# Full-array first-layer products for the first two blocks of a convolution and maxout kernel

## The chip, the cores and the metric

The kernel runs on one core of a Trainium2 chip. The core has four engines that compute: TensorE (PE in the profile; PEld is its loading of weights), VectorE (DVE), ScalarE (ACT) and GpSimd (POOL). SyncE (SP) issues most of the DMAs. SBUF is the core's memory of 128 partitions, PSUM the memory into which TensorE accumulates. The metric is the time of one execution on the device in microseconds (us), as the median of several runs; lower is better.

## The reference

The input x has 8 sequences of 4160 tokens with 192 channels. A causal convolution of width 7 is applied per channel, with weights that a softmax gives for each of 8 heads of 24 channels. A feed-forward layer follows: three matrices of 192 x 768, the largest of the three products for each element, and a matrix of 768 x 192.

```python
# cut to what is computed
w = softmax(weight, axis=-1)                       # 8 heads x 7 taps
x_pad = concatenate([zeros((B, 6, D)), x], axis=1) # causal
out[b, s, h*24 + g] = sum_k w[h, k] * x_pad[b, s + k, h*24 + g]
h = maximum(maximum(out @ w1, out @ w2), out @ w3) # 33280 x 768
return h @ w_out                                   # 33280 x 192
```

## The kernel before

The 33,280 tokens are cut into 65 blocks of 512. With y the convolved block, the kernel uses max(a, b, c) = c + max(a - c, b - c, 0): it computes only the two products y(w1 - w3) and y(w2 - w3), takes relu of the first, then the larger of that and the second, and adds y(w3 w_out) at the end by a merged matrix m16 = w3 w_out.

The 192 channels are three chunks of 64. A product with 64 rows fills half of the 128-row array, so two run beside each other, one in each half: half 0 does w1 - w3, half 1 does w2 - w3. For that, each half of the partitions needs all three chunks of y. The convolution gives each chunk in one half, and the other half is a copy.

The first four blocks are "dense": their convolution (`conv_dense`) leaves channels on partitions at once. The copies into the other half are `cross` (VectorE) and, for block 3, `cross_dma`.

```python
    def conv_dense(t, copies):
        yd = dense[t] = ydp.tile([P, NC, NBLK], FP16, tag="yd", name=f"yd_{t}")   # NC = 3
        for n, slots_ in enumerate((range(4), range(4, 6))):
            ps = psw.tile([P, NBLK], FP32, tag="w", name=f"D{n}_{t}")
            for (q, b, row_lo, rlen, lo, hi, cc) in chunks_of[t]:                 # 5 of up to 103 tokens
                for v in range(2):
                    for g, s in enumerate(slots_):
                        h = (32 * s + 31 * v) // GRP
                        nc.tensor.matmul(ps[32 * g:32 * g + 32, lo:hi], ...)      # L347
            if n == 0:
                copies[0](out=yd[0:HALF, 0, :], in_=ps[0:HALF, :])                # L353
                copies[1](out=yd[HALF:P, 1, :], in_=ps[HALF:P, :])                # L354
            else:
                copies[2](out=yd[0:HALF, 2, :], in_=ps[0:HALF, :])                # L356

    def cross(t, cs=range(NC)):
        for c in cs:
            a, b = (slice(HALF, P), slice(0, HALF))[::-1 if c == 1 else 1]
            nc.vector.tensor_copy(out=yd[a, c, :], in_=yd[b, c, :])               # L363
```

From block 4 on, the convolution (`conv`, L328) leaves tokens on partitions. Its result is written to SBUF as ys (`evac`, L376) and turned by DMA transposes (`turn`, L390). Then the halves are exchanged by `double` (L400): by DMA for blocks 4 and 5, and by GpSimd after that. Blocks 5 and 6 share one turn and one doubling, so do 7 and 8, and so on up to 16; block 4 has its own. Loads of x (`load_x`, L153) and casts (`cast_x`, L183) run some blocks ahead.

```python
    def double(t, by_dma=False):
        yp = dense[t]
        copy = nc.sync.dma_start if by_dma else nc.gpsimd.tensor_copy
        for i in range(2):
            copy(out=yp[HALF * i:HALF * (i + 1), 1, ...], in_=yp[HALF * (1 - i):HALF * (2 - i), 0, ...])
```

The first layer `l1(t, j)` makes 128 of the 768 columns of one block: three 512-column products in each half. ScalarE's relu and VectorE's maximum follow (L482, L483). The second layer `st2` (L532) does 60 products of 192 columns a block; ScalarE and VectorE add its halves (L540, L541).

```python
        for c in range(NC):
            for i in range(2):
                nc.tensor.matmul(ps[i][:], lhsT=wd[HALF * i:HALF * (i + 1), c, P * j:P * (j + 1)],
                                 rhs=y_all(t, i, c), start=(c == 0), stop=(c == NC - 1))   # L475
        # then: r = relu(ps[0]) on ScalarE, h = max(r, ps[1]) on VectorE
```

In the start of the kernel, x of blocks 0 and 1 and the weights are loaded in three parts of 256 columns, the weight differences wd are made, and the layers of blocks 0 and 1 are interleaved. `keep_warm` are matmuls on zeros.

```python
    def load_w(part):
        for st, lo, wsrc in ((w3s, 0, moe_w3), (ws, 0, moe_w1), (ws, HALF, moe_w2)):
            nc.sync.dma_start(out=st[lo:lo + HALF, :, f], in_=...)                # 64 x 3 x 256, L213
    # order on SyncE: load_x(0), load_w(0), load_x(1), load_w(1), load_w(2), wos (L224), load_x(2..5)
    ...
    copy_w3(nc.vector.tensor_copy, 0);  make_wd(0, 1)                             # L284, L280
    conv_dense(0, (ACT, ACT, ACT));     keep_warm(2)
    cross(0, (0,));  make_wd(1, 2, nc.gpsimd);  cross(0, (1, 2))
    cast_dense(1, ...);  copy_w3(nc.vector.tensor_copy, 1);  l1(0, 0)
    conv_dense(1, (ACT, ACT, ACT));  cross(1);  make_wd(2, 4)
    ...                                        # l1 of blocks 0 and 1, casts and transposes of w3
    nc.gpsimd.tensor_copy(out=wo[:], in_=wos[:])                                  # L619
    load_x(6), load_x(7);  l1(0, 5);  make_m(0);  make_m(1)
    cast_dense(2);  l1(1, 4);  st2(0, (5, 5))
    conv_dense(2, ...);  cast_dense(3);  cast_x(4);  cross(2);  l1(1, 5)
    for u in range(1, 6): st2(0, (5 * u + 5, 5 * u + 5))
    ...
    # block 2: after l1(2, 0): conv_dense(3), cross_dma(3), load_x(8), conv(4), evac, turn(4), load_x(9), casts 5, 6
    # block 3: double(4, by DMA), load_x(10), casts 7, 8; after l1(3, 1): conv(5) for blocks 5 and 6, turn(5)
    # block 4: double(5, by DMA), load_x(11), ...
```

Of the kernel before, what the change touches and what calls it, by code (L numbers as in the profile page):

```python
# [28 lines left out]
def kernel(  # L29
# [177 lines left out]
    w3s = const.tile([P, NC, DFF], FP32)  # L207
    PW = 2 * P

    def load_w(part):  # L210
        f = slice(PW * part, PW * (part + 1))
        for st, lo, wsrc in ((w3s, 0, moe_w3), (ws, 0, moe_w1), (ws, HALF, moe_w2)):
            nc.sync.dma_start(out=st[lo:lo + HALF, :, f],  # L213
                              in_=wsrc.rearrange("(c r) f -> r c f", r=HALF)[:, :, f])
# [5 lines left out]
    load_w(0)  # L220
    load_x(1)
    load_w(1)
    load_w(2)
# [5 lines left out]
    for t in range(2, 6):  # L229
        load_x(t)  # L230
# [24 lines left out]
    nc.scalar.activation(out=line[:, 31:31 + KW], in_=wexp[:], func=AF.Relu, scale=wrec[:])  # L255
# [3 lines left out]
    CUT = 25  # L259
    for lo, hi, copy in ((0, CUT, nc.scalar.copy), (CUT, WIN, nc.vector.tensor_copy)):  # L260
        bps = psq.tile([32, hi - lo, NHEAD], FP32, tag="q", name=f"band_{lo}")
        for c in range(lo, hi):
            nc.tensor.matmul(bps[:, c - lo, :], lhsT=line[:, WIN - 1 - c:WIN + 31 - c],
                             rhs=ident16[0:NHEAD, 0:NHEAD], start=True, stop=True)
        for a in range(4):
            copy(out=band[32 * a:32 * a + 32, :, 32 * a + lo:32 * a + hi],
                 in_=bps[:].rearrange("p c h -> p h c"))
    keep_warm(3, psp, "p")
# [3 lines left out]
    w3h = const.tile([HALF, NC, DFF], FP16)  # L272
    wd = const.tile([P, NC, DFF], FP16)
# [4 lines left out]
    def make_wd(j0, j1, eng=nc.vector):  # L278
        f = slice(P * j0, P * j1)
        eng.tensor_sub(out=wd[:, :, f], in0=ws[:, :, f], in1=w3s[:, :, f])  # L280

    def copy_w3(copy, part):
        f = slice(PW * part, PW * (part + 1))
        copy(out=w3s[HALF:P, :, f], in_=w3s[0:HALF, :, f])  # L284

    def cast_w3(part):
        f = slice(PW * part, PW * (part + 1))
        nc.gpsimd.tensor_copy(out=w3h[:, :, f], in_=w3s[0:HALF, :, f])

    def transpose_w3(g):  # L290
        ps = psw.tile([P, 2, D], FP32, tag="w", name=f"pt{g}")
        for k in range(2):
            js = slice(P * (2 * g + k), P * (2 * g + k + 1))
            for c in range(NC):
                nc.tensor.matmul(ps[:, k, HALF * c:HALF * (c + 1)], lhsT=w3h[:, c, js],
                                 rhs=ident16[0:HALF, 0:HALF], start=True, stop=True)
        nc.scalar.copy(out=w3t[:, 2 * g:2 * g + 2, :], in_=ps[:])
# [39 lines left out]
    def conv_dense(t, copies):  # L337


        yd = dense[t] = ydp.tile([P, NC, NBLK], FP16, tag="yd", name=f"yd_{t}")  # L340
        for n, slots_ in enumerate((range(4), range(4, 6))):
            ps = psw.tile([P, NBLK], FP32, tag="w", name=f"D{n}_{t}")
            for (q, b, row_lo, rlen, lo, hi, cc) in chunks_of[t]:
                for v in range(2):
                    for g, s in enumerate(slots_):
                        h = (32 * s + 31 * v) // GRP
                        nc.tensor.matmul(  # L347
                            ps[32 * g:32 * g + 32, lo:hi],
                            lhsT=xz[t][v][0:rlen, q, 32 * s:32 * s + 32],
                            rhs=band[0:rlen, h, cc:cc + hi - lo],  # L350
                            start=(v == 0), stop=(v == 1), tile_position=(0, 32 * g))
            if n == 0:
                copies[0](out=yd[0:HALF, 0, :], in_=ps[0:HALF, :])  # L353
                copies[1](out=yd[HALF:P, 1, :], in_=ps[HALF:P, :])  # L354
            else:
                copies[2](out=yd[0:HALF, 2, :], in_=ps[0:HALF, :])  # L356

    def cross(t, cs=range(NC)):

        yd = dense[t]  # L360
        for c in cs:
            a, b = (slice(HALF, P), slice(0, HALF))[::-1 if c == 1 else 1]
            nc.vector.tensor_copy(out=yd[a, c, :], in_=yd[b, c, :])  # L363

    def cross_dma(t):
        yd = dense[t]
        nc.sync.dma_start(out=yd[HALF:P, 0:NC:2, :], in_=yd[0:HALF, 0:NC:2, :])
        nc.sync.dma_start(out=yd[0:HALF, 1, :], in_=yd[HALF:P, 1, :])
# [24 lines left out]
    def double(t, by_dma=False):  # L393

        if not NDENSE <= t < NB:
            return
        yp = dense[t]
        copy = nc.sync.dma_start if by_dma else nc.gpsimd.tensor_copy
        for i in range(2):
            copy(out=yp[HALF * i:HALF * (i + 1), 1, :, :, :, :].rearrange("p i u k n -> p (i u k n)"),  # L400
                 in_=yp[HALF * (1 - i):HALF * (2 - i), 0, :, :, :, :].rearrange("p i u k n -> p (i u k n)"))
# [11 lines left out]
    def y_all(t, i, c):  # L413
        if t < NDENSE:
            return dense[t][HALF * i:HALF * (i + 1), c, :]
        a = y_row(t, i)
        s0, s1, s2, s3 = (spot(t, i, c, r) for r in range(4))
        assert s3 - s2 == s1 - s0
        return bass.AP(tensor=a.tensor, offset=a.offset + P * s0,
                       ap=[list(a.ap[0]), [P * (s2 - s0), 2], [P * (s1 - s0), 2], [1, P]])  # L420

    def y_tok(t, i, c, s):
        if t < NDENSE:
            return dense[t][HALF * i:HALF * (i + 1), c, P * s:P * (s + 1)]
        a = y_row(t, i)
        return bass.AP(tensor=a.tensor, offset=a.offset + P * spot(t, i, c, s), ap=[list(a.ap[0]), [1, P]])
# [38 lines left out]

    def l1(t, j, pools=((psp, "p"), (psq, "q"))):
# [4 lines left out]
        def product(i, c):  # L471
            if c == 0:
                pool, tag = pools[i]
                ps[i] = pool.tile([P, NBLK], FP32, tag=tag, name=f"l{tag}{i}_{t}_{j}")
            nc.tensor.matmul(ps[i][:], lhsT=wd[HALF * i:HALF * (i + 1), c, P * j:P * (j + 1)],  # L475
                             rhs=y_all(t, i, c), start=(c == 0), stop=(c == NC - 1))

        def top():
            if t not in hs:
                hs[t] = hp.tile([P, NJ, NBLK], FP16, tag="h", name=f"h_{t}")  # L480
            r = rp.tile([P, NBLK], FP16, tag="r", name=f"r_{t}_{j}")
            nc.scalar.activation(out=r[:], in_=ps[0][:], func=AF.Relu)  # L482
            nc.vector.tensor_max(out=hs[t][:, j, :], in0=r[:], in1=ps[1][:])  # L483
            done[t] = j + 1
# [4 lines left out]
        op(top)  # L489
        emit()  # L490

# [88 lines left out]
    copy_w3(nc.vector.tensor_copy, 0)  # L580
    make_wd(0, 1)
    conv_dense(0, (nc.scalar.copy, nc.scalar.copy, nc.scalar.copy))
    keep_warm(2)
    cross(0, (0,))
    make_wd(1, 2, nc.gpsimd)
    cross(0, (1, 2))
    cast_dense(1, (nc.gpsimd.tensor_copy, nc.scalar.copy))
    copy_w3(nc.vector.tensor_copy, 1)
    l1(0, 0)
    meet()  # L590
    cast_w3(0)
    conv_dense(1, (nc.scalar.copy, nc.scalar.copy, nc.scalar.copy))
    cross(1)
    make_wd(2, 4)
    l1(0, 1)
    meet()
    keep_warm(2)
    l1(1, 0)
    meet()
    cast_w3(1)  # L600
    l1(1, 1, WW)
    meet()
    transpose_w3(0)
    copy_w3(nc.gpsimd.tensor_copy, 2)
    l1(0, 2)
    meet()
    cast_w3(2)
    transpose_w3(1)
    make_wd(4, 6, nc.gpsimd)
    l1(0, 3, WW)  # L610
    meet()
    transpose_w3(2)
    l1(1, 2)
    meet()
    l1(1, 3, WW)
    meet()
    l1(0, 4)
    meet()
    nc.gpsimd.tensor_copy(out=wo[:], in_=wos[:])  # L619
    for t in (6, 7):  # L620
        load_x(t)
    l1(0, 5, WW)
    meet()
    make_m(0)
    make_m(1)
    cast_dense(2, (nc.gpsimd.tensor_copy, nc.gpsimd.tensor_copy))
    l1(1, 4)
    meet()
    st2(0, (5, 5))
    meet()  # L630
    conv_dense(2, (nc.scalar.copy, nc.vector.tensor_copy, nc.scalar.copy))
    cast_dense(3, (nc.gpsimd.tensor_copy, nc.gpsimd.tensor_copy))
    cast_x(4)
    cross(2)
    l1(1, 5)
    meet()
    for u in range(1, NJ):
        st2(0, (5 * u + 5, 5 * u + 5))
        meet()
# [7 lines left out]
    for t in range(5, NB):  # L647
        casts[t] = min(NB - 1, casts[t - 1] + (2 if t in (6, 9, 12) else 1))
    loads = {t: min(NB - 1, casts.get(t + 1, 0) + 1) for t in range(4, NB)}
    loads.update({2: 9, 3: 10, 4: 12})  # L650
# [9 lines left out]
    for t in range(2, NB):  # L660
        u = convs_at.get(t, NB)
        late = t > 2 and u < NB
        if t in (3, 4):
            double(t + 1, True)
        if t in (3, 4):
            load_x(t + 7)
# [4 lines left out]
        if t == 2:  # L671
            meet()
            conv_dense(3, (nc.scalar.copy, nc.vector.tensor_copy, nc.scalar.copy))
            cross_dma(3)
            load_x(8)
# [4 lines left out]
            load_x(9)  # L680
# [8 lines left out]
        else:  # L689
            op(lambda t=t: store(t - 2, 0, 4, (nc.sync,)))  # L690
# [54 lines left out]
```

## Time and profile before

| | |
|---|---|
| median of 3 runs | 459.82 us (458.68 to 460.01) |
| span of the profiled run | 458.7 us |
| TensorE busy | 449.6 us, 98% |
| VectorE, ScalarE, GpSimd busy | 359.8, 318.9, 203.4 us |
| granted TensorE clock | 1.00 over the whole span |
| TensorE busy in 25-30, 40-45, 50-55 us | 4.21, 4.11, 3.98 us of 5 |
| the same in 80-85 and 85-90 us | 5.00 and 5.00 of 5 |

A line of the timeline gives start and length in us, the engine (SPq is SyncE's queue of DMA issues), the line of the source, the operation, and the tiles it writes and reads, with the number of instructions merged. A bracket at its end is the idle time of the engine just before it and who ended it. In the chain of waits a piece is start, length and what the end of the program was waiting for at that time. A busy TensorE isn't a TensorE at its peak, since matmuls overlap: the time between the starts of two is what counts.

### The profile page before, as it was taken

To read this page: it belongs to the slowest core of one execution; us is meant where nothing else is said; L and a number is where in the kernel's file an instruction comes from. 1 tells how busy PE (TensorE), PEld (TensorE's weight loads), DVE (VectorE), ACT (ScalarE), POOL (GpSimd) and SP (SyncE) were. 2 spreads that over 40 slices of the span, in tenths; PEclk is the share of its full clock that TensorE was granted. 3 is DMA by queue.
4 is the path that set the end of the run, shared out by engine and by line. 5 is a ranking of instruction groups with operands and counts; after the bars stand their busy time and mean duration, and the time that the engine had idled before them with its cause. 6 is when DMAs were issued, how large, how long until landed. Compare 5 with 4: busy or idle time off the path is not lost.

```text
span 458.7 us, 18657 instructions
## 1 busy us (share of the span) xinstructions
PE 449.6 (98%) x7783; PEld 413.9 (90%) x7783; DVE 359.8 (78%) x616; ACT 318.9 (70%) x609; POOL 203.4 (44%) x223
## 2 busy tenths in 40 slices
PE   8989999999999999999999999999999999999996
PEld 4468799999999999999999999999999999999996
DVE  7767687778878787787878778787878878787775
ACT  5756676667767677776767677676767677676674
POOL 6792166466443464535445354514545452405000
PEclk9999999999999999999999999999999999999999
DMA  8959898897697959879594967759495775525113
GB/s 202 222 134 187 183 212 183 199 208 192 146 178 120 207 140 161 185 122 212 123 210 126 161 182 160 188 110 221 122 190 145 164 176 141 116 89 107 59 64 105
DMA packets 128628, 72.83 MB, mean 159 GB/s; under 512 B 52064, under 2 KB 128415, under 8 KB 128543
## 3 DMA queue, kind: packets, MB, share of 16 engines
q1 hardware_dynamic: 128383, 71.54, 71.5%
q8 instruction: 61, 1.00, 1.0%
q14 instruction: 24, 0.20, 0.1%
q10 hardware_dynamic: 160, 0.10, 0.1%
HBM read 33.28 MB, written 25.56 MB: 128 GB/s over the span
## 4 chain that ended last, share of the span: by engine, by line
PE 89%; DMA 6%; SPq 2%; DVE 1%; issue 1%; POOL 1%; ACT 0%; DVEq 0%; POOLq 0%
PE po L532 34%; PE lq L475 30%; PE lp L475 21%; PE G L328 3%; DMA wos<-in_moe_w_out_dram 2%; DMA yp<-ys 2%; DMA yp<-yp 2%; SPq L213 1%; DVE o L541 0%; SPq L153 0%; DVE yd L363 0%; PE D L347 0%; POOL xz L200 0%; POOL wo L619 0%; DVE yd L354 0%
## 5 line engine op out<-in xcount | busy, mean ns | idle before, releaser
L532 PE MATMUL po<-wo,h 64*128 64x192 f16 x3120 | 336.0, 243 | 0.0
L483 DVE TENSOR_TENSOR h<-r,lq 128x512 f16<-128x512 f16 x386 | 264.6, 686 | 88.1 <-ACT r L482 80.6
L482 ACT ACTIVATE r<-lp 128x512 f16<-128x512 f32 x386 | 230.6, 597 | 115.3 <-PE lp L475 104.0
L475 PE MATMUL lp<-yp,wd 64*128 64x512 f16 x1098 | 295.8, 376 | 1.7 <-DMA yp<-yp 1.0
L475 PE MATMUL lq<-yp,wd 64*128 64x512 f16 x1098 | 295.6, 376 | 0.3 <-DMA yp<-yp 0.3
L532 PEld LDWEIGHTS <-h 64*128 64x128 f16 x3120 | 245.6, 94 | 7.2 <-issue 3.8
L475 PEld LDWEIGHTS <-wd 64*128 64x128 f16 x2340 | 182.0, 94 | 17.8 <-issue 2.7
L183 POOL CAST x<-xf 103x768 f16<-103x768 f32 x122 | 97.5, 828 | 107.9 <-DMA xf<-in_x_dram 84.9
L532 PE MATMUL po<-m,yp 64*128 64x192 f16 x732 | 143.3, 243 | 0.0
L400 POOL COPY yp<-yp 64x1536 f16<-64x1536 f16 x58 | 85.0, 1465 | 104.0 <-DMA yp<-ys 53.3
L541 DVE TENSOR_TENSOR o<-a,po 128x384 f32<-128x384 f32 (+1 forms) x132 | 71.3, 542 | 1.7 <-PE po L532 1.1
L532 PEld LDWEIGHTS <-yp 64*128 64x128 f16 x732 | 67.3, 94 | 0.7
L540 ACT COPY a<-po 128x384 f32<-128x384 f32 (+1 forms) x132 | 61.7, 468 | 2.1 <-PE po L532 1.9
L376 ACT CAST ys<-G 128x384 f16<-128x384 f32 x61 | 26.3, 482 | 11.1 <-PE G L328 11.1
L376 DVE CAST ys<-G 128x384 f16<-128x384 f32 x61 | 31.0, 550 | 1.0 <-PE G L328 1.0
L328 PE MATMUL G<-x,band 39*32 39x192 f16 (+2 forms) x1216 | 17.9, 231 | 1.2 <-issue 1.2
L328 PEld LDWEIGHTS <-band 39*32 39x32 f16 x1216 | 11.3, 91 | 6.2 <-issue 6.1
L475 PE MATMUL lq<-yd,wd 64*128 64x512 f16 x60 | 16.7, 377 | 0.2 <-DVE h L483 0.2
L475 PE MATMUL lp<-yd,wd 64*128 64x512 f16 x60 | 16.7, 377 | 0.0
L347 PEld LDWEIGHTS <-xz 112*32 112x32 f16 x240 | 5.1, 107 | 3.3 <-POOL xz L200 1.3
L532 PE MATMUL po<-m,yd 64*128 64x192 f16 x48 | 7.1, 244 | 0.0
L347 PE MATMUL D<-band,xz 112*32 112x103 f16 (+1 forms) x240 | 6.7, 229 | 0.3
(51 smaller groups left out, 72.6 us busy)
## 6 DMA issues: line engine op xcount, KB each, us to landing
xf<-in_x_dram SPq DMA_DIRECT2D x113, 234.0 KB
out_dram<-o SPq DMA_DIRECT2D x62, 384.0 KB
xf<-in_x_dram SPq DMA_DIRECT2D x7, 204.8 KB
xf<-in_x_dram SPq DMA_DIRECT2D x3, 420.0 KB
ws<-in_moe_w_dram SPq DMA_DIRECT2D x6, 192.0 KB
yp<-ys SPq DMA_TRANSPOSE x62
out_dram<-o SPq DMA_DIRECT2D x5, 192.0 KB
w3s<-in_moe_w_dram SPq DMA_DIRECT2D x3, 192.0 KB
```

The source lines that it names most:

```text
L183: nc.gpsimd.tensor_copy(out=x16s[t0][0:K, :, :, u, r, :].rearrange("p h j c -> p j h c"), in_=xf[0:K, 4 * r:4 * r + 4, :].rearrange("p j ( ...
L213: nc.sync.dma_start(out=st[lo:lo + HALF, :, f], in_=wsrc.rearrange("(c r) f -> r c f", r=HALF)[:, :, f])
L328: nc.tensor.matmul(G[2 * (k // per) + i][TOK * j:TOK * (j + 1), k % per, :], lhsT=band[row, h, HALF * i + LAP:HALF * i + KR], rhs=x16s[t0] ...
L347: nc.tensor.matmul(ps[32 * g:32 * g + 32, lo:hi], lhsT=xz[t][v][0:rlen, q, 32 * s:32 * s + 32], rhs=band[0:rlen, h, cc:cc + hi - lo], star ...
L376: copy(out=slots[t][:, i % 2, :, :, GRP * h0:GRP * (h0 + per)].rearrange("p u r (h c) -> p h (u r) c", c=GRP), in_=G[i][:].rearrange("p h ...
L400: copy(out=yp[HALF * i:HALF * (i + 1), 1, :, :, :, :].rearrange("p i u k n -> p (i u k n)"), in_=yp[HALF * (1 - i):HALF * (2 - i), 0, :, : ...
L475: nc.tensor.matmul(ps[i][:], lhsT=wd[HALF * i:HALF * (i + 1), c, P * j:P * (j + 1)], rhs=y_all(t, i, c), start=(c == 0), stop=(c == NC - 1))
L482: nc.scalar.activation(out=r[:], in_=ps[0][:], func=AF.Relu)
L483: nc.vector.tensor_max(out=hs[t][:, j, :], in0=r[:], in1=ps[1][:])
L532: nc.tensor.matmul(ps[b0, i][:, s % 2, :], lhsT=a, rhs=b, start=first, stop=last)
L540: nc.scalar.copy(out=a[:, ss, :], in_=ps[s0, 0][:, ss, :])
L541: nc.vector.tensor_add(out=outs[t][:, s0:s + 1, :], in0=a[:, ss, :], in1=ps[s0, 1][:, ss, :])
```

## The change

In blocks 0 and 1 the first two chunks are multiplied as one product of 128 rows in the full array, once with w1 - w3 and once with w2 - w3. Only the third chunk is still a pair of halves. So these blocks need no crossed copies of y, except that the third chunk stands in both halves, which the dense convolution now writes by itself (four groups of 32 columns in place of two). The weights are loaded in a layout of 128 channels and 64 channels, with more and smaller DMAs.

Blocks 2 and 3 keep the pairs of halves. For their middle products they need chunk 1 in half 0 and chunk 0 in half 1, two copies instead of three, and the same exchange in the weights (`cross_wd`, once). Block 3's copies move from DMA to GpSimd. The doublings of blocks 4 and 5 move from DMA to GpSimd as well. The loads of x stand later in SyncE's queue by about a block, but block 6 is loaded at the start. The steps of l1 for blocks 0 and 1 come in pairs of tiles, with ScalarE's and VectorE's part placed by hand. Three idle matmuls are put between those that make the band of the convolution, and there are fewer elsewhere.

```diff
-    w3s = const.tile([P, NC, DFF], FP32)
+    w3s = const.tile([P, 2, DFF], FP32)
+    def load_wa(f):
+        for st, n, wsrc in ((w3s, 0, moe_w3), (ws, 0, moe_w1), (ws, 1, moe_w2)):
+            nc.sync.dma_start(out=st[:, n, f], in_=wsrc[0:P, f])
+    def load_wb(f):
+        for st, lo, n, wsrc in ((w3s, 0, 1, moe_w3), (ws, 0, 2, moe_w1), (ws, HALF, 2, moe_w2)):
+            nc.sync.dma_start(out=st[lo:lo + HALF, n, f], in_=wsrc[P:D, f])
     load_x(0)
-    load_w(0)
+    load_wa(slice(0, PW))
     load_x(1)
-    load_w(1)
-    load_w(2)
+    load_wb(slice(0, PW))
+    load_wa(slice(PW, 2 * PW))
+    load_wb(slice(PW, DFF))
+    load_wa(slice(2 * PW, DFF))
     ... wos ...
-    for t in range(2, 6):
+    for t in range(2, 7):
         load_x(t)
...
-    nc.scalar.activation(out=line[:, 31:31 + KW], in_=wexp[:], func=AF.Relu, scale=wrec[:])
+    nc.vector.tensor_scalar_mul(out=line[:, 31:31 + KW], in0=wexp[:], scalar1=wrec[:])
...
+            if c % 13 == 0:
+                nc.tensor.matmul(beside[:], lhsT=idle[HALF:P, 0:P], rhs=idle[HALF:P, :], start=True, stop=True)
...
-    keep_warm(3, psp, "p")
+    keep_warm(2, psp, "p")
...
+    def cross_wd():
+        nc.vector.tensor_copy(out=wd[0:HALF, NC, :], in_=wd[HALF:P, 0, :])
+        nc.scalar.copy(out=wd[HALF:P, NC, :], in_=wd[0:HALF, 1, :])
...
-        for n, slots_ in enumerate((range(4), range(4, 6))):
+        for n, slots_ in enumerate(((0, 1, 2, 3), (4, 5, 4, 5))):
...
-            if n == 0:  (three copies, see above)
+            copies[n](out=yd[:, 2 * n, :], in_=ps[:])
...
-    def cross_dma(t): ...
-    def double(t, by_dma=False):
+    def double(t):                       # always nc.gpsimd.tensor_copy
...
+    def l1_dense(tiles):
+        for t, j, pools in tiles:
+            for i, (pool, tag) in enumerate(pools):
+                nc.tensor.matmul(ps[t, j, i][:], lhsT=wd[:, i, P * j:P * (j + 1)], rhs=dense[t][:, 0, :],
+                                 start=True, stop=False)
+        for t, j, _ in tiles:
+            for i in range(2):
+                nc.tensor.matmul(ps[t, j, i][:], lhsT=w_of(i, NC - 1, j), rhs=y_all(t, i, NC - 1),
+                                 start=False, stop=True)
...
+    make_wd(0, 0, 2)
+    make_wd(1, 0, 2)
+    conv_dense(0, (ACT, DVE))
+    keep_warm(1)
+    copy_w3(DVE, 0, 2)
+    make_wd(2, 0, 2)
+    cast_dense(1, (nc.gpsimd.tensor_copy, ACT))
+    a, b = l1_dense([(0, 0, PQ), (0, 1, PQ)])
+    a()                                   # relu and maximum of (0, 0); b() those of (0, 1)
+    cast_w3(0, 2)
+    conv_dense(1, (ACT, ACT))
+    make_wd(0, 2, 4)
+    make_wd(1, 2, 4)
+    b()
+    copy_w3(ACT, 2, 6)
+    make_wd(2, 2, 6)
+    ... l1_dense [(1,0),(1,1)], [(0,2),(0,3)], [(1,2),(1,3)], [(0,4),(0,5)], then
     nc.gpsimd.tensor_copy(out=wo[:], in_=wos[:])
+    cast_dense(2), cast_dense(3), cast_x(4)
+    ... l1_dense [(1,4),(1,5)]
     make_m(0)
     make_m(1)
+    st2(0, (10, 10))
+    conv_dense(2, (ACT, DVE))
+    cross_wd()
     cross(2)
+    ... the rest of st2(0)
...
-    loads.update({2: 9, 3: 10, 4: 12})
+    loads.update({2: 8, 3: 10})
...
-            double(t + 1, True)
-        if t in (3, 4):
-            load_x(t + 7)
+            double(t + 1)
...
-            cross_dma(3)
-            load_x(8)
+            cross(3, nc.gpsimd.tensor_copy)
             conv(u, PQ)
             evac(u, 0)
             evac(u, 1, nc.vector.tensor_copy)
             turn(4)
-            load_x(9)
+            load_x(7)
+            load_x(8)
...
-            op(lambda t=t: store(t - 2, 0, 4, (nc.sync,)))
+            op(lambda t=t: (store(t - 2, 0, 4, (nc.sync,)), load_x(9) if t == 3 else None))
```

## The prediction

> **What bounds the kernel now.** I first read the page's header and its chain of work that ended last.
>
> ```profile
> span 458.7 us, 18657 instructions
> PE 449.6 (98%) x7783; PEld 413.9 (90%) x7783; DVE 359.8 (78%) x616; ACT 318.9 (70%) x609; POOL 203.4 (44%) x223
> PE 89%; DMA 6%; SPq 2%; DVE 1%; issue 1%; POOL 1%; ACT 0%; DVEq 0%; POOLq 0%
> ```
>
> The chain is TensorE for 89%. What is not TensorE can be gained, so I read the same chain in order of time from 0 to 60 us, its long pieces:
>
> ```profile
> 8.33 10.12 DMA wos<-in_moe_w_out_dram
> 18.51 1.15 POOL wo L619
> ...
> 22.26 1.06 POOL xz L200 x4
> ...
> 35.18 4.76 DMA yp<-ys
> 40.02 5.01 DMA yp<-yp
> ...
> 45.24 5.14 DMA yp<-ys
> ...
> 50.92 3.10 DMA yp<-yp
> 54.07 0.39 PE lq L475
> ```
>
> Columns are start, length, what. All DMA lies before 54.07 us. After that the chain is TensorE alone, so the change pays only through the time at which block 5's first product starts in both halves, 54.07 now. In the timeline of TensorE two convolutions of the steady part (62.55 and 76.06) are 13.5 us apart for two blocks, 6.75 a block.
>
> How much is there to win? TensorE's need from the first product (8.74) to 54.07, in columns: 30 layer-1 groups of three paired 512-column steps at 0.214 us (starts 27.02, 27.24, 27.45) are 19.3; four second layers of 30 paired steps of 192 columns at about 0.082 are 9.8; three dense convolutions of 1.45 are 4.4; three other convolutions 2.2; transposes, the merged matrices, idle matmuls and the start of later work about 3.5. The sum is 39.2 of 45.3 us. So 6 us, 1.3%, is the most that this stretch hides; 2% would be 9.2 us.
>
> The timeline of TensorE shows where it stands still late in this stretch:
>
> ```profile
> 30.60 0.55 PE L328 MATMUL G<-x,band 39*32 39x48 f16 x50 [1.25 <-issue]
> ...
> 45.08 0.39 PE L475 MATMUL lp<-yp,wd 64*128 64x512 f16 x1 [0.97 <-DMA yp<-yp]
> ...
> 53.18 0.37 PE L475 MATMUL lp<-yp,wd 64*128 64x512 f16 x1 [0.72 <-ACT a L540]
> ...
> 54.07 0.39 PE L475 MATMUL lq<-yp,wd 64*128 64x512 f16 x1 [0.30 <-DMA yp<-yp]
> ```
>
> The last three waits, some 2 us, belong to the swaps that are done by DMA. The queue that issues them explains their lateness:
>
> ```profile
> 33.77 2.60 SPq L390 DMA_TRANSPOSE yp<-ys  x2
> ...
> 40.02 1.44 SPq L400 DMA_DIRECT2D yp<-yp  x2
> 41.56 1.00 SPq L153 DMA_DIRECT2D xf<-in_x_dram  x2
> 42.61 0.44 SPq L571 DMA_DIRECT2D out_dram<-o  x1
> 43.14 4.70 SPq L390 DMA_TRANSPOSE yp<-ys  x2
> ```
>
> Block 4's transposes are issued at 33.77, though ScalarE and VectorE had written ys by 31.8. The swap waits at the queue's head until they land (40.02) and holds back block 5's transposes to 43.14, whose ys was ready at 40.95.
>
> **What the Trainium skill says.** "DMA: Bandwidth & Descriptors", Rules for kernel authors: a DMA that reads what an earlier one wrote must wait for its completion before it is issued. The trace agrees, with that stop at 40.02. The same page, Anatomy of one DMA, gives about 2 us of fixed cost per DMA (fitted for DMAs issued from GpSimd); the swaps here, 5.01 and 3.10 us on the chain, are above it. "SBUF — State Buffer", Who interferes with whom: VectorE copies in two-port modes and GpSimd lock each other out. The trace fits: the crossed copies of 64x512 on VectorE take 287 ns at best and up to 797, the long ones beside GpSimd's casts. "TensorE: Matmul & The Clock Gate", Back-to-back issue gap, gives 512/2.4+2.5 = 216 ns a warm full-array matmul, as the 0.214 of a pair here.
>
> **The change, part by part.**
>
> 1. Full-array products. A group was three paired steps of 512 columns. It becomes two full-array steps and one paired step: 3 x 0.214 = 0.64 us before and after. TensorE gains nothing by it.
>
> 2. Crossed copies. Blocks 0 and 1 lose six copies of VectorE: of the nine, 0.29 + 0.94 + 0.93 are in this part, 2.2 us with their gaps. Two evacuations take the place of three, and one of them goes to VectorE (0.69). VectorE also gets all of the weight differences: it had 1.5 us for half of them, GpSimd 3.2 for the rest, so +1.5. The w3 copies shrink from 2.0 to about 0.3, for ScalarE takes the larger (about 0.55). VectorE's sum: -2.2 + 0.7 + 1.5 - 1.7 = -1.7 us.
>
> 3. When do blocks 0 and 1 end? SyncE's weight issues grow from 9 to 15, at 0.63 us each, so the third chunk of the first weights, the ninth DMA, is issued by 6.5 instead of 3.7. As many bytes had landed by 9.35 before (block 1's x, which GpSimd casts from then on), so I put it at 9.4. From there VectorE is the pacer: w3 copy and difference to 10.0; first maximum at 11.3 to 11.9 (11.63 before); then 12 maxima at 0.64 (the pitch of the unwaited ones from 17.94 to 19.82) = 7.7 plus 2.0 of differences, plus one wait of about 0.8 for ScalarE, which must evacuate block 1 first: 11.5 + 10.5 = 22. The last products, held back by PSUM buffers that the maxima free, end near 21.0.
>
> 4. The output weights. They are issued at 12.2 instead of 8.3, but the bytes ahead of them are the same (3.2 MB with them) and the page has 202 to 222 GB/s here. I put the landing at 18, before 18.46, and wo at 19.2. GpSimd has no memset after it any more (1.9 us), so block 2's casts end at 20.8 and not at 24.9. That is ahead of TensorE: this wait goes.
>
> 5. But block 2 gets new steps. From 21.0: merged matrices 1.3, first maxima of the second layer 0.8, dense convolution 1.5 plus some 0.15 for the 20 added matmuls, at 24.7. Then VectorE alone evacuates (0.69), crosses wd (about 0.5 for 64x768) and crosses two chunks (0.3 to 0.6 each): 24.7 + 2.3 = 27.0. TensorE has 1.6 us of second layer meanwhile and then waits. Block 2's first product starts at 27.0, as it does today (27.02). The early gain is spent here: 0, give or take 1 us.
>
> 6. Block 4. Its ys is ready at 31.8 again. With no load and no crossing DMA ahead, the transposes go at 31.9 instead of 33.8 and land at 36.5 to 37.5. GpSimd doubles in 2 x 0.75 us (half of the 1465 ns that a 64x1536 copy takes): 38 to 39, where the DMA ended at 45.0. TensorE needs it at 44.1. The wait of 1 us goes.
>
> 7. Block 5. The load of block 9 stands ahead of its transposes in SyncE's queue, and that load waits for a memset that stands on GpSimd behind the doubling of block 4 and the casts of blocks 7 and 8. Doubling to 38.5, two casts of 1.6 each and a memset (0.25) to 42, the memset of 0.6 to 42.7, the load's issue to 43.7: transposes at 43.7, not earlier than 43.14 today. They land 6.3 us after issue in most of the later cases (63.87 to 70.13, 90.88 to 97.23; 4.4 at best): 49.5 to 50. The doubling by GpSimd takes 2.99 for both halves: 52.5 to 53. That against 54.07 is 1.0 to 1.5 us gained; TensorE comes there at about 50.8 and stands still for some 2 us.
>
> The sum: 0 (point 5) + 1.2 (point 7). Point 6's microsecond isn't added to it, for block 5's wait swallows it. I allow another 0.4 for the 1.25 us of "issue" in the convolution at 29.35, which has no cause in the trace and may fall elsewhere. From 459.82 that gives 458.2.
>
> **The rivals.** (a) VectorE and block 2's crossings are faster than I put them (every copy at its 0.29), so block 2 starts 1.5 us earlier and all that follows with it, and the transposes land in 4.5 us. For it: the crossed copies without GpSimd beside them are short. Against it: GpSimd casts blocks 2 to 4 at just that time. It makes 455 to 456.5. (b) The queue of SyncE becomes the bound: fifteen weight issues delay the third chunk and wo by 2 us, or block 5's transposes wait for GpSimd's memset until 45. For it: the issues of 0.6 us follow one another without a gap up to 8.9 us now, and point 7's chain has no slack. Against it: the DMAs are then busy with earlier bytes anyway. It makes 460 to 461.5. (c) Later loads of x starve the steady part. For it: casts already wait for loads there. Against it: those waits, up to 7 us on GpSimd, don't reach TensorE today. It would add 1 to 3 us.
>
> **Range and chances.** The middle, 458.2, takes point 7 at its middle. Rival (a) gives the lower end, 455.8, (b) or a little of (c) the upper, 460.8. The three runs before span 1.3 us by themselves. Faster by 2% needs 9.2 us, more than the stretch hides: 2%. Slower by 2% needs starvation in every pair of blocks: 2%. The rest, 96%, is within 2%.
>
> **What would show it.** Right: the chain still TensorE after about 53; block 2's first product near 27; no wait before block 4; a wait of 1 to 3 us before block 5 released by a GpSimd copy; SyncE's second transposes close behind a load of x near 43.7. Wrong: block 2's first product before 25.5 or after 28 (points 3 to 5); block 5's transposes before 42 (point 7); idle TensorE after 60 us (rival c); wo's cast after 21 (point 4).

## The result and the profile after

The changed kernel takes 463.56 us in the median against 459.91 for the kernel before: a ratio of 1.0079 with a 95% interval of 1.0051 to 1.0107. It is slower by 3.65 us, less than 2%. The prediction was 458.2 us (455.8 to 460.8): a small gain was expected, and there is a small loss, 5.4 us from it.

The header and the chain of waits on the page of the changed kernel:

```profile
span 461.4 us, 18767 instructions
PE 453.4 (98%) x7832; PEld 414.2 (90%) x7832; DVE 359.4 (78%) x617; ACT 317.0 (69%) x605; POOL 204.2 (44%) x227
PE 96%; DVE 1%; issue 1%; DMA 1%; ACT 1%; POOL 0%; ACTq 0%; POOLq 0%; DVEq 0%
```

DMA has fallen from 6% of the chain to 1%, as the change meant it to, and yet the time is longer. The 96% of TensorE don't say that it did more work: its stall ahead of block 5 is short against the whole span, and a TensorE at half its clock also counts as TensorE.

The same chain in order of time, start, length and what, around block 5's start:

```profile
49.46 3.14 DMA yp<-ys
52.85 1.38 issue
54.23 1.48 POOL yp L411
55.75 0.37 PE lq L494
```

Where transposes and a swap by DMA ended the waits, there are transposes that land at 52.6 and a doubling by GpSimd behind them. Block 5 starts in both halves at 55.75, not 54.07. SyncE's queue says why so late:

```profile
32.60 2.60 SPq L402 DMA_TRANSPOSE yp<-ys  x2
35.30 3.56 SPq L153 DMA_DIRECT2D xf<-in_x_dram  x5
38.91 1.21 SPq L597 DMA_DIRECT2D out_dram<-o  x2
46.33 0.81 SPq L153 DMA_DIRECT2D xf<-in_x_dram  x2
47.23 3.47 SPq L402 DMA_TRANSPOSE yp<-ys  x2
```

From 40.1 to 46.3 SyncE issues nothing. Block 5's ys was ready at 42.3 (ScalarE and VectorE write it from 40.99 to 42.26), but its transposes go only at 47.23. The load of block 9's x stands ahead of them and waits. The timeline of GpSimd shows for what:

```profile
38.53 1.71 POOL L411 COPY yp<-yp 64x768 f16<-64x768 f16 x2 [1.74 <-DMA yp<-ys]
41.39 1.59 POOL L183 CAST x<-xf 103x768 f16<-103x768 f32 x2 [1.15 <-PE G L350]
42.94 0.25 POOL L180 MEMSET xf<- 7x192 f32 x1
44.07 1.60 POOL L183 CAST x<-xf 103x768 f16<-103x768 f32 x2 [0.89 <-DMA xf<-in_x_dram]
45.73 1.08 POOL L126 MEMSET xf<- 32x576 f32 x2
52.71 2.99 POOL L411 COPY yp<-yp 64x1536 f16<-64x1536 f16 x2 [5.89 <-DMA yp<-ys]
```

Block 9's buffer gets its zeros from the first of the two memsets at 45.73. That stands behind the doubling of block 4, which waits for block 4's transposes, and behind the casts of blocks 7 and 8, whose x was loaded late (35.3 to 38.9, after those transposes). The bracket at 41.39 names TensorE's convolution, but in experiment 2, where x comes earlier, the same cast doesn't wait for that convolution to end; so it was x that it waited for. It is a ring: SyncE waits for GpSimd, and GpSimd for DMAs that SyncE had issued late.

The last part is the clock. The same profile in stretches of 2 us; the columns are busy time and number of instructions on PE, PEld, DVE, ACT and POOL, then the granted clock, the DMA share and GB/s:

```profile
52.00:54.00 2.00, 0.56 (x9) 0.42 (x5) 1.22 (x2) 0.97 (x2) 1.29 (x1) 1.00 0.85 195
54.00:56.00 2.00, 0.84 (x10) 0.50 (x11) 0.56 (x1) 0.00 (x0) 1.88 (x3) 1.00 1.30 235
56.00:58.00 2.00, 2.00 (x24) 1.72 (x22) 0.69 (x1) 0.88 (x2) 2.00 (x3) 0.65 1.75 159
58.00:60.00 2.00, 2.00 (x19) 1.68 (x16) 0.69 (x1) 0.52 (x2) 0.90 (x2) 0.50 0.70 149
```

TensorE is idle for most of 52 to 56 us. In 56 to 60 us it is "busy" for all of the time and does 24 and 19 matmuls in 2 us where 50 to 52 us has 33: the clock has fallen to half. All four executions of the changed kernel have a mean clock of 0.996, which a fall of this size gives, though the mean doesn't say where it came.

**Where the time is lost.** From block 4's first product to the convolution of block 9 every kernel has the same work, so this stretch compares across profiles without the start. Its ends are, before,

```profile
45.08 0.39 PE L475 MATMUL lp<-yp,wd 64*128 64x512 f16 x1 [0.97 <-DMA yp<-yp]
...
62.48 0.75 PE L328 MATMUL G<-x,band 39*32 39x96 f16 x64
```

and after, with block 5's first products in each half between them:

```profile
45.26 0.38 PE L494 MATMUL lp<-yp,wd 64*128 64x512 f16 x1
...
54.23 0.37 PE L494 MATMUL lp<-yp,wd 64*128 64x512 f16 x1 [1.66 <-POOL yp L411]
55.75 0.37 PE L494 MATMUL lq<-yp,wd 64*128 64x512 f16 x1 [0.94 <-POOL yp L411]
...
65.83 0.75 PE L350 MATMUL G<-x,band 39*32 39x96 f16 x64
```

Before it is 17.40 us. After it is 20.57 us, 3.17 more. Of that, block 5's second half starts 1.50 us later within the stretch (10.49 after its beginning, 8.99 before), and from there to the convolution it is 10.08 us instead of 8.41, 1.67 more, which is the clock.

### The profile page after: what moved, and what is told of

Its sections match the earlier page's. It is cut to its first block, busy times and chain, and to the rows that moved or that the text cites. A ratio compares the mean times of both kernels' runs of the same rounds, so it can differ in the third digit from the quotient of the medians.

```text
span 461.4 us, 18767 instructions
## 1 busy us (share of the span) xinstructions
PE 453.4 (98%) x7832; PEld 414.2 (90%) x7832; DVE 359.4 (78%) x617; ACT 317.0 (69%) x605; POOL 204.2 (44%) x227
## 4 chain that ended last, share of the span: by engine, by line
PE 96%; DVE 1%; issue 1%; DMA 1%; ACT 1%; POOL 0%; ACTq 0%; POOLq 0%; DVEq 0%
PE po L558 36%; PE lq L494 31%; PE lp L494 21%; PE G L350 3%; PE D L369 1%; DMA yp<-ys 1%; PE lw L510 0%; PE lq L510 0%; PE lp L514 0%; PE pt L317 0%; PE lp L510 0%; POOL yp L411 0%; PE idle L241 0%; PE band L270 0%; ACT L256 0%
## 5 line engine op out<-in xcount | busy, mean ns | idle before, releaser
L494 PEld LDWEIGHTS <-wd 64*128 64x128 f16 x2268 | 179.0, 94 | 13.4 <-issue 2.7
L411 POOL COPY yp<-yp 64x1536 f16<-64x1536 f16 (+1 forms) x62 | 89.6, 1445 | 88.2 <-DMA yp<-ys 48.6
L350 PEld LDWEIGHTS <-band 39*32 39x32 f16 x1216 | 11.3, 91 | 4.9 <-issue 4.7
L494 PE MATMUL lq<-yd,wd 64*128 64x512 f16 x36 | 9.9, 376 | 0.3 <-issue 0.3
L494 PE MATMUL lp<-yd,wd 64*128 64x512 f16 x36 | 9.9, 376 | 0.0
L126 POOL MEMSET xf<- 32x576 f32 (+1 forms) x7 | 6.2, 916 | 0.2
```

Source lines behind the costliest of these rows:

```text
L126: nc.gpsimd.memset(xf[TOK:HALF, 0 if t < XBUF else NQ:NR, :], 0.0)
L350: nc.tensor.matmul(G[2 * (k // per) + i][TOK * j:TOK * (j + 1), k % per, :], lhsT=band[row, h, HALF * i + LAP:HALF * i + KR], rhs=x16s[t0] ...
L411: nc.gpsimd.tensor_copy(out=yp[HALF * i:HALF * (i + 1), 1, :, :, :, :].rearrange("p i u k n -> p (i u k n)"), in_=yp[HALF * (1 - i):HALF * ...
L494: nc.tensor.matmul(ps[i][:], lhsT=w_of(i, c, j), rhs=y_all(t, i, c), start=(c == 0), stop=(c == NC - 1))
```

## The experiments

The *queue theory* says that the loss is this wait of block 5's transposes, with the clock that falls after it. The *start theory* says that it comes from the start (block 2's first product at 28.93 instead of 27.02) and is passed on. Ratios are to the kernel before, run on the same chip; brackets give the 95% interval. The changed kernel's own ratio, 1.0079, is from four executions of each kernel. Single profiles scatter, so times of executions are read from the ratios and causes from the profiles.

**1. Block 9's load behind block 5's transposes**

```diff
-            op(lambda t=t: (store(t - 2, 0, 4, (nc.sync,)), load_x(9) if t == 3 else None))
+            op(lambda t=t: store(t - 2, 0, 4, (nc.sync,)))        # load_on(3) loads 9 and 10 after turn(5)
```

> The changed kernel with one thing moved: the load of block 9's x goes behind block 5's transposes in SyncE's queue instead of ahead of them. Queue theory (the loss is block 5's transposes held from 41.9 to 47.2 us by a load that waits for a memset on GpSimd, and TensorE's clock that falls in the stall that follows): transposes issued at about 42, no stall over 0.5 us before block 5, the clock stays at 1.00 in 54 to 60 us, and the time falls from 463.6 by 1.7 (block 5 in both halves at 54.0 or earlier) + 1.7 (clock) + up to 1.7 more (block 4 ends at 52.3) to 458.5 to 460.2. Start theory (the loss is the start: block 2's first product at 28.93 instead of 27.02, passed on to the end): the time stays within 0.7 us of 463.6.

Measured: 459.41 us, ratio 0.9971 (0.9951 to 0.9992). One moved load makes the changed kernel faster than the one before. Its queue of SyncE, and the first of the stretches in which TensorE had stood still:

```profile
44.23 3.99 SPq L402 DMA_TRANSPOSE yp<-ys  x2
49.86 2.87 SPq L153 DMA_DIRECT2D xf<-in_x_dram  x4
```

```profile
52.00:54.00 2.00, 2.00 (x34) 1.94 (x31) 1.75 (x3) 1.61 (x4) 1.66 (x2) 1.00 0.94 184
54.00:56.00 2.00, 2.00 (x34) 1.94 (x31) 1.44 (x3) 1.53 (x4) 0.00 (x0) 1.00 1.19 229
```

The ends of the stretch:

```profile
47.61 0.38 PE L494 MATMUL lp<-yp,wd 64*128 64x512 f16 x1
...
63.49 0.75 PE L350 MATMUL G<-x,band 39*32 39x96 f16 x64
```

Here block 4 began at 47.61 us, 2.35 later than in the changed kernel (TensorE had stood 1.78 us with the mark "issue" in block 3's convolution), and the transposes still go 3.0 earlier. They don't land faster for it: from their issue to GpSimd's doubling it is 6.5 us, against 5.5 in the changed kernel, so the gain isn't that of a quieter DMA. No stall follows, the clock stays at 1.00, and the stretch from block 4 to block 9's convolution (63.49) is 15.88 us, 4.69 less than in the changed kernel and 1.52 less than before. The queue theory's number holds; the start theory, which expected no change, falls as the main cause. The whole of this execution was the slowest of its 20, 463.22 us: TensorE stood another 2.10 us in block 6 (70.95), again with the mark "issue".

**2. Earlier loads of blocks 7 and 8**

```diff
     cast_x(4)
+    load_x(7)
+    load_x(8)
...
             turn(4)
-            load_x(7)
-            load_x(8)
```

> The changed kernel with the loads of x of blocks 7 and 8 issued right after block 4's cast is put on GpSimd (about 28 us), not behind block 4's transposes (35.3 us); block 9's load still stands ahead of block 5's transposes. Queue theory: GpSimd casts blocks 7 and 8 right after the doubling of block 4 and reaches the memset 1 to 2 us sooner, so that block 5's transposes go at 45.3 to 46.3 instead of 47.2; the stall before block 5 gets shorter by as much, and the time falls by 1 to 3 us (the upper end if the clock doesn't fall any more) to 460.6 to 462.6. If instead the casts wait for TensorE's convolution and not for the load, below 1 us. Start theory: no change.

Measured: 462.13 us, ratio 1.0018 (0.9991 to 1.0045). GpSimd now casts without waits (block 7 at 41.39, directly after the doubling and while TensorE is still in its convolution, 40.89 to 41.64; block 8 at 43.24), so the casts had waited for the loads. But block 4's transposes landed later, and the ring opened only 0.8 us sooner. GpSimd, then SyncE's queue:

```profile
39.62 1.70 POOL L411 COPY yp<-yp 64x768 f16<-64x768 f16 x2 [4.84 <-DMA yp<-ys]
41.39 1.59 POOL L183 CAST x<-xf 103x768 f16<-103x768 f32 x2
```

```profile
45.50 0.80 SPq L153 DMA_DIRECT2D xf<-in_x_dram  x2
46.39 2.55 SPq L402 DMA_TRANSPOSE yp<-ys  x2
```

In this profile the transposes took 7.3 us to land (to 53.65), so block 5 started no earlier (56.69), and yet the stretch is 1.14 us shorter than in the changed kernel, for the clock stayed at 1.00. By the ratios, 1.0018 against 1.0079 with intervals that don't overlap, the early loads are worth 2.8 us, as expected (1 to 3); this profile's stretch shows 1.14 of them. So the late loads are part of the ring, and the intervals are too wide for a closer size.

**3. Idle matmuls in the stall**

```diff
     for t in range(2, NB):
+        if t == 5:
+            meet()
+            keep_warm(8)
         l1(t, 0)
```

> The changed kernel with eight idle matmuls (8 x 0.216 = 1.7 us) put on TensorE in the stall ahead of block 5. They can't make block 5 start earlier. If the fall of the clock to 0.5 from about 56.7 to 60 us is a cost of its own (products 0.43 us apart for some 4 us, 1.66 us lost by comparing 55.75 to 65.89 with 54.07 to 62.55 before), the clock stays at 1.00 and the time falls by about 1.7 to 461.9. If the clock isn't set by the stall, or costs nothing, the time stays at 463.6 or gets longer.

Measured: 462.75 us, ratio 1.0039 (1.0019 to 1.0059), some 1.8 us below the changed kernel's ratio, though the two intervals overlap a little. (`meet()` also puts what is left of the second layer ahead of the idle matmuls.) The clock:

```profile
54.00:56.00 2.00, 1.05 (x16) 0.84 (x17) 0.00 (x0) 0.40 (x1) 1.94 (x3) 1.00 0.95 230
56.00:58.00 2.00, 2.00 (x35) 1.59 (x31) 1.38 (x2) 1.07 (x3) 2.00 (x3) 1.00 1.27 93
58.00:60.00 2.00, 2.00 (x35) 1.59 (x31) 1.65 (x3) 1.49 (x4) 1.03 (x2) 1.00 1.09 214
```

Block 5 still waits until 54.95 in both halves. From there to the convolution of block 9 it is 8.54 us, against 10.08 in the changed kernel. So the fall of the clock is a cost beside the stall. That these matmuls are what prevents it isn't shown by the one profile: in experiments 2 and 7, which have the stall and no idle matmuls, the clock didn't fall either, and the same distance is 8.40 in both. In experiment 4 it did, and the distance is 10.07. The fall cost 1.67 us in these two profiles, and it doesn't come each time.

**4. The start undone**

```diff
-    nc.vector.tensor_scalar_mul(out=line[:, 31:31 + KW], in0=wexp[:], scalar1=wrec[:])
+    nc.scalar.activation(out=line[:, 31:31 + KW], in_=wexp[:], func=AF.Relu, scale=wrec[:])
-            if c % 13 == 0:
-                nc.tensor.matmul(beside[:], ...)
-    keep_warm(2, psp, "p")
+    keep_warm(3, psp, "p")
-    for t in range(2, 7):              # load_x
+    for t in range(2, 6):              # load_x(6) after cast_w3(0, 2)
```

> The changed kernel with three things at the start undone: the scaled softmax line is written by ScalarE again (VectorE took 1.25 us for it, ending with GpSimd's second memset), no idle matmuls beside the band's, and block 6's memset and load come later, so that GpSimd does two memsets and not three while VectorE casts x of block 0. Expected in the start: the first dense convolution at about 6.4 instead of 7.8 us. Start theory: block 2's first product moves from 28.9 to about 27.3 and the time falls by 1.5 to 2 us to about 461.8. Queue theory: block 4's chain begins at most 0.8 us sooner, so 0.3 to 1.4 us, 462.2 to 463.3.

Measured: 462.33 us, ratio 1.0032 (1.0004 to 1.0060). The first dense convolution starts at 6.46 instead of 7.80 us, block 2's first product at 26.67 instead of 28.93. Block 4 starts at 45.41 in this profile, no earlier than in the changed kernel, because TensorE stood 1.79 us in block 3's convolution with the mark "issue" (0.37 in the changed kernel's profile); the ring and the fall of the clock are there as before (the stretch is 21.26 us). By the ratios, 1.0079 and 1.0032, the start is a second cost of about 2 us; their intervals overlap, so this run alone doesn't show it.

**5. The load's place and the start together**

The edits of 1 and 4.

> The changed kernel with the edits of the first and the fourth experiment together: block 9's load behind block 5's transposes, and the start undone (line by ScalarE, no idle matmuls beside the band's, block 6's memset later). Queue theory with the start as a second, additive cost: no stall before block 5, the first product of block 2 at about 27, and the ratio to the kernel before falls from 0.997 (first experiment) by another 0.003 to about 0.994. If the start is swallowed by a later wait, 0.997 as in the first. Start theory alone: 1.003, as in the fourth.

Measured: 458.11 us, ratio 0.9929 (0.9909 to 0.9950). By the ratios the two add up, as expected: 0.997 and another 0.004, with intervals that only just part. The stretch is 15.88 us again. The profile shows nothing of the second gain: block 2's first product comes at 28.86, not near 27. The first dense convolution is early (6.44), but then TensorE waits for the third chunk's weights, and its clock falls to 0.50 in 12 to 14 us:

```profile
11.22 0.61 PE L511 MATMUL lp<-yd,wd 64*128 64x512 f16 x1 [2.40 <-DVE wd L284]
```

**6. The same with early loads of blocks 7 and 8**

The edits of 1, 2 and 4.

> The same as the run beside it, with the loads of blocks 7 and 8 also issued early. Queue theory: with the transposes no longer behind a load that waits for GpSimd, earlier loads have nothing left to give: the same ratio within 0.002, about 0.994. If the later loads are a cost of their own (traffic beside the transposes of block 5), 0.001 to 0.003 lower.

Measured: 458.83 us, ratio 0.9948 (0.9932 to 0.9965). With the ring open, the earlier loads give nothing.

**7. Only the line by ScalarE**

The first two lines of experiment 4's edit.

> The changed kernel with only the scaled softmax line back on ScalarE. If VectorE's 1.25 us for these 8 x 7 elements are a wait for GpSimd's memset (it ends with the second memset at 4.42), ScalarE writes it in 0.3 us, the band's first matmul goes from 4.49 to about 3.9 and the first dense convolution from 7.80 to 7.2; VectorE's first cast of x still ends only with the third memset, at about 5.8. If the operation itself is slow on VectorE, the cast doesn't show the same wait.

Measured: 460.38 us in a single execution, so only the profile is read. The line no longer waits, the first dense convolution starts at 7.35 (7.80 in the changed kernel), and the cast of x still waits for the third memset. VectorE, then GpSimd, in the changed kernel:

```profile
3.19 1.25 DVE L259 TENSOR_SCALAR line<-wexp,wrec 8x7 f16<-8x7 f32 x1
3.98 0.46 DVE L261 MEMSET xz<- 128x480 uint32 x2
4.39 2.22 DVE L200 CAST xz<-xf 112x240 f16<-112x240 f32 x6
```

```profile
1.73 4.03 POOL L126 MEMSET xf<- 32x1536 f32 x3
```

The 56 elements of the line are done at 4.44, when the second of the three memsets of 1.34 us ends (1.73 + 2 x 1.34 = 4.41). The first of the six casts takes 1510 ns, from 4.39 to just behind the end of the third memset (5.76); the longest of the six takes 290 in the kernel before, which has two memsets there, and 284 in experiment 4, which puts the third later:

```profile
4.70 1.00 DVE L200 CAST xz<-xf 112x240 f16<-112x240 f32 x6 [0.53 <-DMA xf<-in_x_dram]
```

**8. The kernel before with GpSimd's swaps**

```diff
-            double(t + 1, True)
-        if t in (3, 4):
-            load_x(t + 7)
+            double(t + 1)                # and loads 10, 11 follow the transposes by load_on
```

> The kernel before with the swaps of blocks 4 and 5 done by GpSimd and the loads of blocks 10 and 11 behind the transposes; its layout, its paired halves and its crossed copies stay. Queue theory: the waits before blocks 4 and 5 (0.97 + 0.72 + 0.30 us, and the time between them) go, transposes of block 5 at about 41 to 41.5, and the ratio is 0.995 to 0.997; then the full-array products are not what gains. If the layout is what gains in the first experiment: 0.999 to 1.001.

Measured: 460.22 us, ratio 0.9972 (0.9950 to 0.9993). Block 5's transposes go at 40.22, there is no wait before blocks 4 and 5, and the distance from block 4's first product (43.60) to the convolution of block 9 (59.48) is 15.88 us, as in experiments 1 and 5. So the gain behind block 4 belongs to the swaps and the order of the queue, and needs no full-array product. In this profile the mark "issue" comes twice, 1.10 us in block 4's convolution and 1.36 in block 9's.

**9. The third chunk's weights ahead of block 1's x**

The edits of 5, and:

```diff
-    load_x(1)
     load_wb(slice(0, PW))
+    load_x(1)
```

> The fastest kernel so far (block 9's load behind block 5's transposes, start undone; 0.993 of the kernel before), with the three weight DMAs of the third chunk issued ahead of block 1's x. There TensorE waits 2.4 us for the third chunk (landed at 9.8 to 10.4) and its clock falls to 0.5 from about 11.4 to 14 us. Expected if the third chunk's place in the queue is the cause: landed at about 8, the paired products of the first tiles at about 9.5 instead of 11.2, no fall of the clock there, ratio about 0.990 to 0.992. If block 1's x, now later, takes its place as the bound (its casts from 10.5 instead of 9.6): the same 0.993.

Measured: 457.27 us, ratio 0.9934 (0.9906 to 0.9962). VectorE's copy of the third chunk no longer waits (9.08 instead of 9.77), and the paired products start at 10.25 instead of 11.22, not at 9.5. The clock stays at 1.00 there, and block 2's first product comes at 26.66 instead of 28.86. By the ratio it is the same as experiment 5 all the same; the interval still holds the 0.990 to 0.992 that had been expected, so a gain of 1 us is neither shown nor excluded.

**10. The first experiment with the swaps by DMA**

```diff
-            double(t + 1)
+            double(t + 1, True)          # nc.sync.dma_start, as before the change
```

> The first experiment (changed kernel with block 9's load behind block 5's transposes) with the swaps of blocks 4 and 5 by DMA again, as before the change. If the swaps on GpSimd are a gain of their own: block 4's swap by DMA takes 3 to 5 us instead of 1.7 after the transposes land, it holds block 5's transposes by 0.5 to 1 us, and the ratio is 0.999 to 1.002 instead of 0.997. If only the order in SyncE's queue matters: 0.997 as in the first.

Measured: 464.91 us, ratio 1.0079 (1.0047 to 1.0112): all that experiment 1 gained is lost, more than expected. The queue, and the first product of block 5:

```profile
41.27 3.71 SPq L402 DMA_TRANSPOSE yp<-ys  x2
45.24 1.74 SPq L153 DMA_DIRECT2D xf<-in_x_dram  x4
47.42 1.11 SPq L412 DMA_DIRECT2D yp<-yp  x2
```

```profile
56.24 0.58 PE L495 MATMUL lp<-yp,wd 64*128 64x512 f16 x1 [4.28 <-issue]
```

Block 4's swap held the transposes of block 5 little (41.27). But block 5's swap was issued behind the loads of blocks 9 and 10. The bracket names no releaser; ScalarE and VectorE do nothing in 54 to 56 us, so the wait is taken to be for the swap, which this product reads. By this reading the swap took from 47.42 to 56.24, 8.8 us, where GpSimd takes 2.99. The clock fell here too (0.55 to 0.50 in 54 to 60 us). So with this order of the queue the swaps on GpSimd are a gain of the change, and the load's place is its fault. What a swap by DMA ahead of those loads would cost isn't shown here; in the kernel before, where the swap stands ahead of the load, experiment 8 gained 0.003 without it.

## Why the prediction was wrong

- *What bounds the kernel, and where the change can pay.* Right: TensorE without waits behind block 5, all differences before it. The stretch from block 4 to block 9's convolution was worth 1.5 us to a kernel without the waits (15.88 against 17.40), and 1.0 to 1.5 had been predicted of it. The bracket of the wait of 0.72 us at 53.18 names ScalarE, not a swap as the working had it; experiment 8, with no swap of blocks 4 and 5 by DMA, has none of the three waits.
- *Point 1, full-array products.* Right for the warm array: the two products of a full-array pair are 0.21 us apart (14.35 and 14.56). At the first tiles they are 0.43 apart (10.04, 10.47, 10.90, 11.32): the array was cold. The working had taken one speed for all. The Trainium skill, "TensorE: Matmul & The Clock Gate", What's actually happening, has the cold clock at half the warm one, which these two distances show; the granted clock in the profile reads 1.00 there and doesn't. This is not the change alone: in experiment 10, whose start is the same, the first two are 0.22 apart (9.93, 10.15).
- *Point 3, the end of blocks 0 and 1.* Wrong: the first maximum came at 13.09, not at 11.3 to 11.9, and the last products at 23.39, not near 21.0. The term left out is the start itself. The working began at the landing of the third chunk and took the convolution ahead of it as it was, though the diff moves the line to VectorE and adds a memset. The Trainium skill, "SBUF — State Buffer", Who interferes with whom (VectorE in a two-port mode and GpSimd block each other), had been cited for the crossed copies and not applied to these lines; the trace agrees with it at 1510 against 290 ns. With the start undone (experiment 4) the first maximum comes at 11.31 and the last products at 21.14, as predicted. The ratios of experiments 1, 4 and 5 put about 2 us on the start, but single executions scatter as much: block 2's first product comes at 27.57 to 28.93 in the five profiles that have the changed start, and at 26.66 to 28.86 in the four that have it undone.
- *Point 4, the output weights.* Right: landed at 18.1, wo cast at 18.10 and block 2's casts done at 21.16 (20.8 predicted). No wait for them remains.
- *Point 5, block 2's new steps.* 28.93 instead of 27.0, but all of that comes from point 3. From the last products to block 2's first the working has 6.0 us and the trace 5.5 (23.39 to 28.93): cross_wd took 0.36 and a crossed copy 0.29, the fast end.
- *Point 6, block 4.* Right that the wait goes: none at 45.26. The transposes were issued at 32.60 (31.9 predicted) but landed at 38.5, not at 36.5 to 37.5, and the doubling ended at 40.24, not at 38 to 39.
- *Point 7, block 5.* This step failed. The ring was seen ("the load of block 9 stands ahead of its transposes in SyncE's queue"), and its terms were each put too small: doubling of block 4 done at 40.24 instead of 38.5 (1.7), the cast of block 7 waits for its load (1.15), that of block 8 too (0.89). Together 3.7, and the transposes went at 47.23 instead of 43.7. So block 5 started in both halves at 55.75, where 52.5 to 53 had been predicted. The loads of blocks 7 and 8 had been taken as there in time, although they were issued after the transposes of block 4. Experiment 1 takes this one wait away and turns 1.0079 into 0.9971.
- *The fall of the clock.* Not in the prediction at all. A stall of "some 2 us" was counted as 2 us; it was 3.0 (20.57 - 15.88 - 1.67) and cost 1.67 us beyond itself. Block 5's later start and the clock together are 4.4 to 4.9 of the 5.4 us by which the time was missed. Why the clock fell after this stall (waits of 1.66 and 0.94 us) and not after a longer one (2.16 and 0.93 in experiment 2) is not shown. In the Trainium skill, "TensorE: Matmul & The Clock Gate", What's actually happening, the clock follows the activity in a window of some 3.4 us that runs freely, which would agree with a fall in some profiles and not in others; no run here shows the window.
- *The rivals.* (b) is what happened, "block 5's transposes wait for GpSimd's memset until 45": its mechanism is right and its size, 460 to 461.5, was too small by the clock and by the start. The other half of (b), output weights 2 us late, didn't come (18.1). Of (a) the copies were as fast as it said, but block 2 wasn't early. (c) didn't come: TensorE is busy for all of 60 to 90 us.

What stays open is the mark "issue" of 0 to 1.8 us in the convolutions of blocks 3 and 4 (0.37 after, 1.25 before, 1.78, 1.64, 1.79 and 0.18 in experiments 1, 2, 4 and 5). With the 2.10 us in block 6 of experiment 1 it shifts single profiles by as much as the effects sought, and no experiment aimed at it. Nor is the full-array layout sized by itself: experiment 5 against 8 (0.9929 and 0.9972) has it, but with the start and the loads changed as well, and the intervals touch.

## What to carry to other kernels

SyncE's queue issued in order and passed every wait on. Before a load is put ahead of a transfer that the critical path needs, ask what the load itself waits for: here a memset, behind two casts that waited for two late loads. When work goes from DMA to an engine, follow all that stands in that engine's order, and put loads for later work behind the urgent transfer. The stall of 3.0 us on TensorE cost half as much again by its clock, though not in every execution, so compare distances between the same two pieces of work and not busy shares.

## What the runs showed that had not been expected

- A memset of GpSimd held two VectorE operations until it ended: one of 8 x 7 elements (1.25 us, where ScalarE takes 0.30) and a cast (1510 ns for 290). VectorE's own memsets weren't held: in the kernel before, two of them beside GpSimd's take 0.97 us together.
- The granted clock in the profile is 1.00 in the first 13 us, while full-array matmuls are 0.427 us apart until 11.3; only the distances show that it ran at half speed there. Later falls are recorded (0.50 in 58 to 60 us).
- A swap by DMA in SBUF took 8.8 us behind two blocks' loads of x in the same queue, as the wait of its reader shows it, and 3.1 to 5.0 on the chain of the kernel before.
